# Decode attention on one core: the value loads move from SyncE's queue to GpSimd's

## The chip, the core and the metric

The kernel runs on one core of a Trainium2 chip. The metric is the device time of one execution in microseconds. Three runs of the kernel before gave 1303.39, 1303.53 and 1303.58 us; the median is 1303.53 us. One execution was profiled. The engines are called as the profile calls them: PE (TensorE, matrix products), PEld (its weight loads), DVE (VectorE), ACT (ScalarE), POOL (GpSimd) and SP (SyncE, which here only issues transfers). A "q" behind a name (SPq, ACTq) is that engine's instruction queue, where transfers are issued.

## The reference

One decoding step of grouped-query attention for two tokens, gated by a small MLP; all tensors are 32-bit floats.

```python
xn = layernorm(x)                                   # x: 2 x 1 x 512
q  = (xn @ wq) -> 2 x 32 heads x 128
k, v = caches of 2 x 8 key heads x 32768 x 128, each used by 4 query heads
p  = softmax(q k^T / sqrt(128));  o = p v
s  = o.reshape(2, 4096) @ wo                        # 4096 x 512
g  = silu(relu(xn @ w1 + b1)**2 @ w2 + b2)          # 512 -> 1792 -> 512
out = x + s * g
```

The caches are nearly all of the data: 16 streams (batch x key head) of 16.8 MB of keys and as much of values, 537 MB of the 561 MB that the core reads.

## The kernel before

**Tiling.** A stream s (of 16) has 32768 keys. Its keys K come as two loads of 8.4 MB and its values V as two loads of 8.4 MB, each 128 partitions of 65,536 bytes in one run. Load m of the keys and load j of the values are numbered over all streams, 0 to 31; stream s owns 2s and 2s+1 of both. Every key load is worked through in two quarters q (4 to a stream).

**Buffers.** `kring` has three slots of 32 KB a partition. A key load takes two neighbouring slots: even loads slots 0 and 1, odd loads slots 1 and 2. So the next key load may start when the quarter in the shared slot 1 has been read, which is always the first quarter to be worked on: `load_k(m)` waits for the mark `transposed(2m-2)`. `vbuf` holds a single value load: `load_v(j)` waits until PE has read all of load j-1 (semaphore `pv`, counted by `PV`).

**Work of a quarter.** DVE transposes it from `kring` into `kt` in two instructions (line 309). PE multiplies each half by the masked query `qz` into `ps_s` (line 270). ACT copies the scores out to `sc` (line 333).

**Work of a stream.** After four quarters DVE adds the parts and takes the maximum (line 315), PE spreads it (line 288), DVE makes the bias (line 318), ACT takes the exponential (line 336), PE transposes the probabilities into `pT_ps` (line 299) and ACT copies them to `pTh` (line 343). Then PE multiplies the values by them into `o_ps` (line 280). Values are consumed one stream after their keys.

**Order on each engine.** PE runs a loop over s from 1 to 15: scores of the first two quarters of stream s, values 2s-2, scores of the last two quarters, values 2s-1, then the maximum (288), the transposition of the finished output of stream s-1 (292) and the probabilities (299). It is in order: nothing passes a wait. DVE runs four quarters of transposes, then the maximum, the bias, the sum of the output (485), its reduction (328) and its scaling into `ho` (329), then the sums for the next stream (321, 322). The bias waits for PE, and PE comes to it only after values 2s-1. So the transposes of stream s+1 stand behind values 2s-1.

POOL has two small pieces in a stream: `keep(s-1)`, which copies `ho` into `oT` (line 493) and waits for DVE's line 329, and `set_q(s+1)`, which makes the next masked query (line 246).

**Transfers.** All large loads are issued by SP (line 84, a helper), in program order: weights and the first keys, then in turn a key load and a value load. Each issue stands behind its wait, and the next issue behind it. At the end the last pair of value loads goes to `kring` and to `vbuf`, and the pieces of `wo` to `kring`.

Of the kernel before, what the change touches and what calls it, by code (L numbers as in the profile page):

```python
# [52 lines left out]
def gqa_decode_kernel(nc, x, kc, vc, wq, wo, w1, b1, w2, b2, out):  # L53
# [17 lines left out]
    def sb(name, *shape):  # L71
        return nc.alloc_sbuf_tensor(name, (P,) + shape, F32).ap()

    def bank(name, n=1):
# [3 lines left out]
    SP, ACT, DVE, POOL, TE = (Lane(nc, e, n) for e, n in (  # L78
        (nc.sync, "sp"), (nc.scalar, "act"), (nc.vector, "dve"), (nc.gpsimd, "pool"), (nc.tensor, "pe")))
    tensor, vector, scalar, gpsimd, sync = nc.tensor, nc.vector, nc.scalar, nc.gpsimd, nc.sync  # L80

    def load(lane, dst, src, sem, *marks):
        lane.wait(*marks)
        return sem.after(lane.eng.dma_start(dst, src))  # L84

    def dma(name):
        return Count(nc, name, 16)

    kring = sb("kring", 3 * SLOT, DH)
    vbuf = sb("vbuf", RUN, DH)  # L90
    kt = [sb(f"kt{y}", SLOT, 64) for y in range(2)]

    def rows(cache, s):
        hkv, b = divmod(s, B)
        return cache[b, hkv]
# [5 lines left out]
    def v_rows(j):  # L101
        s, u = divmod(j, 2)
        return rows(vc, s)[u * P * RUN:(u + 1) * P * RUN].rearrange("(p r) d -> p r d", p=P)
# [11 lines left out]
    v_sem = dma("v")  # L115
    KT = [Count(nc, f"kt_{y}") for y in range(2)]
    PA = [Count(nc, f"pa_{y}") for y in range(2)]
    PV = Count(nc, "pv")
# [8 lines left out]
    def load_k(m):  # L127
        a = m % 2
        return load(SP, kring[:, a * SLOT:(a + 2) * SLOT, :], k_rows(m), k_sems[a], transposed(max(2 * m - 2, -1)))
# [114 lines left out]
    def set_q(s):  # L244
        hkv, b = divmod(s, B)
        return POOL(lambda: gpsimd.tensor_tensor(
            qz.rearrange("p e (x h) -> p e x h", h=REP),
            qT[:, b, hkv].rearrange("p h e -> p e h")[:, :, None, :].to_broadcast([P, 4, 8, REP]),
            bm[:, None, :, None].to_broadcast([P, 4, 8, REP]), op=ALU.mult),
            *((have_qT, have_bm) if s == 0 else (PA[1].at(4 * s + 1),)), on=QZ if s else None)  # L250
# [143 lines left out]
    mlp_done = t  # L394

    def load_v(j):
        load(SP, vbuf, v_rows(j), v_sem, PV.at(j) if j else mlp_done)

    load_v(0)
    load_k(3)  # L400
    load_v(1)

    first_keys(3)
    first_scores(3)
# [86 lines left out]
    def keep(s):  # L491
        hkv, b = divmod(s, B)
        return POOL(lambda: gpsimd.tensor_copy(oT[:, b, hkv * REP:(hkv + 1) * REP], ho), (HO.sem, s + 1))  # L493

    for s in range(1, NS):
        for m in (2 * s, 2 * s + 1):
            if m + 2 < NH:
                load_k(m + 2)
                load_v(m)
        kept = keep(s - 1)  # L500
        if s + 1 < NS:
            set_q(s + 1)


    L = NH - 2
# [110 lines left out]
```

## Time and profile before

| | before |
|---|---|
| median of 3 runs | 1303.53 us (1303.39 to 1303.58) |
| span of the profiled execution, first to last instruction | 1302.6 us, 0.93 us under the median |
| busy share of the span: PE, DVE, ACT, POOL | 49%, 48%, 10%, 1% |
| busy share of the 16 DMA engines | 99.6% in SP's queue |
| read from memory | 561.01 MB, 431 GB/s over the span |
| granted clock of PE, mean | 0.785 |

Busy time is the sum of an engine's instructions; issuing and waiting are not counted. The share of a DMA queue is the time that its packets took on 16 DMA engines. A packet here is the run of one partition (65,536 bytes for a key or value load) or a small completion. In a row of the timeline the columns are the start in us, the duration in us, engine, line, operation, what it writes and reads with the tile's size, the count of merged instructions, and in brackets the idle time of the engine ahead of it with what ended it.

### The profile page before, as it was taken

How to read it: one execution, taken by the hardware profiler on the slowest of the kernel's cores; microseconds unless marked ns; L12 is line 12 of the kernel's file. 1: busy time of each engine (PE TensorE's matmuls, PEld its weight loads, DVE VectorE, ACT ScalarE, POOL GpSimd, SP SyncE). 2: the span in 40 equal slices, each digit the busy share in tenths (PEclk: the TensorE clock that was granted, in tenths of full speed). 3: DMA queues.
4: the chain of work that ended last, by engine and by line, in shares of the span. 5: the costliest groups of instructions: out<-in, count | busy, mean ns of one | idle time of the engine just before them, and what ended most of it. 6: DMA issues, size and time to landing. Idle time of an engine off the chain costs nothing.

```text
span 1302.6 us, 10806 instructions
## 1 busy us (share of the span) xinstructions
PE 639.7 (49%) x4710; PEld 175.6 (13%) x4710; DVE 619.0 (48%) x305; ACT 128.6 (10%) x262; POOL 11.9 (1%) x41
## 2 busy tenths in 40 slices
PE   3555444555535455544536543444653444554368
PEld 1111110111101011110101111111110111111014
DVE  2565553436555344655435555343655534455410
ACT  0111011111001011000111101011100101101010
POOL 0000000000000000000000000000000000000000
PEclk9778677878767787777788777678877778877789
DMA  9999999999999999999999999999999999999998
GB/s 419 418 448 423 441 427 435 431 437 433 431 437 427 443 427 441 429 441 427 439 427 437 433 431 437 427 443 427 441 429 441 427 439 427 439 431 429 441 425 356
DMA packets 10703, 561.14 MB, mean 431 GB/s; under 512 B 1199, under 2 KB 1219, under 8 KB 1478
## 3 DMA queue, kind: packets, MB, share of 16 engines
q1 hardware_dynamic: 10656, 560.99, 99.6%
q8 instruction: 6, 0.10, 0.0%
q10 hardware_dynamic: 38, 0.02, 0.0%
q14 instruction: 3, 0.02, 0.0%
HBM read 561.01 MB, written 0.00 MB: 431 GB/s over the span
## 4 chain that ended last, share of the span: by engine, by line
DMA 77%; DVE 12%; issue 10%; PE 1%; SPq 0%; DVEq 0%
DMA kring<-in_A_k_cache 73%; DVE kt L309 12%; DMA kring<-in_A_v_cache 2%; DMA kring<-in_A_wo 2%; PE o_ps L280 1%; PE acc_ps L533 0%; PE pj_ps L540 0%; SPq L84 0%; DVEq L308 0%; PE acc_ps L411 0%
## 5 line engine op out<-in xcount | busy, mean ns | idle before, releaser
L309 DVE STREAM_TRANSPOSE kt<-kring 128x4096 f32<-128x4096 f32 x128 | 557.6, 4414 | 449.4 <-DMA kring<-in_A_k_cache 449.4
L270 PE MATMUL ps_s<-kt,qz 128*32 128x512 f32 x2048 | 333.5, 779 | 603.4 <-DVE kt L309 603.4
L280 PE MATMUL o_ps<-vbuf,pTh 128*16 128x512 f32 x1984 | 227.5, 612 | 1.8 <-DMA vbuf<-in_A_v_cache 1.8
L270 PEld LDWEIGHTS ps_s<-kt,qz 128*32 128x32 f32 x2048 | 67.8, 128 | 845.1 <-issue 669.9
L333 ACT ACTIVATE sc<-ps_s,halves 128x512 f32<-128x512 f32 x64 | 46.6, 729 | 866.5 <-PE ps_s L270 866.5
L280 PEld LDWEIGHTS o_ps<-vbuf,pTh 128*16 128x16 f32 x1984 | 57.8, 101 | 178.0 <-issue 158.6
L343 ACT COPY pTh<-pT_ps 64x256 f32<-64x256 f32 x128 | 46.9, 366 | 39.6 <-PE pT_ps L299 21.6
L315 DVE CUSTOM_DVE_ANT_0 sc<-sc 128x1024 f32<-128x1024 f32 x16 | 19.6, 1225 | 54.9 <-ACT sc L333 54.9
L318 DVE CUSTOM_DVE_ANT_0 junk<-mx_ps,other 128x128 f32<-128x128 f32 x16 | 4.7, 292 | 82.1 <-PE mx_ps L288 82.1
L336 ACT ACTIVATE sc<-sc,nm 128x1024 f32<-128x1024 f32 x16 | 18.4, 1149 | 108.9 <-DVE nm L318 108.9
L328 DVE TENSOR_REDUCE hr<-fin_ps 128x4 f32<-128x64 f32 x16 | 3.6, 225 | 48.5 <-PE fin_ps L292 48.5
L292 PE MATMUL fin_ps<-ident,o_sb 128*128 128x128 f32 x64 | 10.5, 286 | 17.4 <-DVE o_sb L485 17.2
L348 ACT COPY o_sb<-o_ps 128x512 f32<-128x512 f32 x15 | 8.8, 586 | 97.2 <-PE o_ps L280 97.2
L299 PE MATMUL pT_ps<-ident,sc 128*128 128x128 f32 x128 | 17.5, 282 | 0.0
L299 PEld LDWEIGHTS pT_ps<-ident,sc 128*128 128x128 f32 x128 | 15.3, 147 | 0.0
L280 PE MATMUL o_ps<-kring,pTh 128*16 128x512 f32 x64 | 9.3, 749 | 9.0 <-DMA kring<-in_A_v_cache 9.0
L493 POOL COPY oT<-ho 128x4 f32<-128x4 f32 x15 | 2.8, 188 | 1147.2 <-DVE ho L329 1147.2
L210 PE MATMUL pT_ps<-vbuf,xnT 128*32 128x512 f32 x64 | 8.5, 693 | 7.4 <-DMA vbuf<-in_A_wq 7.4
L227 DVE COPY kt<-pT_ps 128x512 f32<-128x512 f32 x8 | 5.0, 683 | 13.2 <-PE pT_ps L210 13.2
L540 PE MATMUL pj_ps<-ident 128*128 128x128 f32 x88 | 10.8, 278 | 0.0
L540 PEld LDWEIGHTS pj_ps<-ident 128*128 128x128 f32 x88 | 10.1, 192 | 1.9 <-issue 1.9
L485 DVE TENSOR_TENSOR o_sb<-o_sb,o_ps 128x512 f32<-128x512 f32 x15 | 10.2, 682 | 0.0
(90 smaller groups left out, 105.5 us busy)
## 6 DMA issues: line engine op xcount, KB each, us to landing
kring<-in_A_k_cache SPq DMA_DIRECT2D x4, 4096.0 KB, 23.8
vbuf<-in_B_w SPq DMA_DIRECT2D x2, 3584.0 KB, 28.5
kring<-in_A_wo SPq DMA_DIRECT2D x1, 4096.0 KB, 41.2
kring<-in_A_wo SPq DMA_DIRECT2D x1, 2304.0 KB, 25.5
kring<-in_A_wo SPq DMA_DIRECT2D x1, 1024.0 KB, 27.6
kring<-in_A_wo SPq DMA_DIRECT2D x1, 512.0 KB, 28.4
vbuf<-in_A_v_cache SPq DMA_DIRECT2D x31, 30.1
kring<-in_A_k_cache SPq DMA_DIRECT2D x30, 29.8
```

The costliest lines, as they stand in the source:

```text
L270: i = tensor.matmul(ps_s[32 * g:32 * g + 32, :], qz[:, 2 * y + e, :], kt[y][:, g * NO:(g + 1) * NO, 32 * e:32 * e + 32], start=(y == 0 and ...
L280: mm_ = tensor.matmul(o_ps[32 * g:32 * g + 16, :], pTh[:, 2 * g + c, 2 * i:2 * i + 2, :, :].rearrange("p o y h -> p (o y h)"), vt[:, lo:lo ...
L292: t = tensor.transpose(fin_ps[:, i * P:(i + 1) * P], o_sb[:, i * DH:(i + 1) * DH], ident)
L299: t = tensor.transpose(pT_ps[:, k // 4, (k % 4) * P:(k % 4 + 1) * P], p[:, k * P:(k + 1) * P], ident)
L309: KT[y].after(vector.transpose(kt[y], k_slot(q)[:, :, 64 * y:64 * y + 64]))
L315: return DVE(lambda: vector.tensor_tensor_reduce(scf[0], scf[0], scf[1], 1.0, -3.4e38, ALU.add, ALU.max, rm), mark, on=on)
L333: ACT(lambda: scalar.mul(sc[c][:, :, :, u], ps_s.rearrange("p (o w) -> p o w", w=32), halves[:, c:c + 1]), *marks, on=EV)
L336: return ACT(lambda: scalar.activation(scf[0], scf[0], AF.Exp, bias=nm, scale=SCALE, accum_out=l), mark, on=on)
L343: i = scalar.copy(pTh[64 * a:64 * a + 64, :, :, y, :], v[64 * y:64 * y + 64, :, :, a0, a, :])
L348: scalar.copy(o_sb, o_ps).then_inc(OE.sem, 32)
L485: DVE(lambda: vector.tensor_add(o_sb, o_sb, o_ps), on=OSR)
L540: tensor.matmul(pj_ps[:, 0:P], ident, ident, start=True, stop=True)
```

## The change

Value loads 0 to 29 are issued from POOL's instruction queue instead of SP's; SP keeps the key loads, the last pair of value loads and the weights. The waits are the same ones: a value load still waits until `vbuf` has been read, a key load until its slots have been read. What is new is that neither queue stands behind the other's waits, and that the value loads stand in POOL's program order, at two places: value load 2s-1 ahead of `keep(s-1)`, and value load 2s behind `keep(s-1)` and `set_q(s+1)`.

```diff
     def load_v(j):
-        load(SP, vbuf, v_rows(j), v_sem, PV.at(j) if j else mlp_done)
+        load(POOL, vbuf, v_rows(j), v_sem, PV.at(j) if j else mlp_done)
 
     load_v(0)
     load_k(3)
-    load_v(1)
...
     for s in range(1, NS):
+        load_v(2 * s - 1)
         for m in (2 * s, 2 * s + 1):
             if m + 2 < NH:
                 load_k(m + 2)
-                load_v(m)
         kept = keep(s - 1)
         if s + 1 < NS:
             set_q(s + 1)
+            load_v(2 * s)
```

SP's order where the steady part begins, before. `kring<-in_A_k_cache` is a key load, `vbuf<-in_A_v_cache` a value load, `vbuf<-in_B_w` a weight of the MLP.

```order
5 L84 DMA vbuf<-in_B_w 128x7168
6 L84 DMA kring<-in_A_k_cache 128x8192 x2
7 L84 DMA vbuf<-in_A_v_cache 128x16384
8 L84 DMA kring<-in_A_k_cache 128x16384
9 L84 DMA vbuf<-in_A_v_cache 128x16384
10 L84 DMA kring<-in_A_k_cache 128x16384
11 L84 DMA vbuf<-in_A_v_cache 128x16384
12 L84 DMA kring<-in_A_k_cache 128x16384
```

And now, up to the end of the streams:

```order
5 L84 DMA vbuf<-in_B_w 128x7168
6 L84 DMA kring<-in_A_k_cache 128x8192 x2
7 L84 DMA kring<-in_A_k_cache 128x16384 x29
8 L84 DMA kring<-in_A_v_cache 128x16384
9 L84 DMA vbuf<-in_A_v_cache 128x16384
10 L84 DMA kring<-in_A_wo 128x8192
```

The strict turn of keys and values is gone from SP: 29 key loads follow one another, each with its own wait.

POOL's order over the first streams, the difference (lines of the kernel after are one less behind the edit). `qz<-qT,bm` is `set_q`, `oT<-ho` is `keep`.

```order
 L246 TENSOR_TENSOR qz<-qT,bm 128x128
-L422 MEMSET oR 128x1024
+L84 DMA vbuf<-in_A_v_cache 128x16384
+L421 MEMSET oR 128x1024
 L246 TENSOR_TENSOR qz<-qT,bm 128x128
-L493 COPY oT<-ho 128x4
+L84 DMA vbuf<-in_A_v_cache 128x16384
+L492 COPY oT<-ho 128x4
 L246 TENSOR_TENSOR qz<-qT,bm 128x128
-L493 COPY oT<-ho 128x4
+L84 DMA vbuf<-in_A_v_cache 128x16384 x2
+L492 COPY oT<-ho 128x4
```

In a steady stream POOL now has `keep`, `set_q`, value load 2s, value load 2s+1, and again `keep`: the even load stands behind two pieces of work, the odd one directly behind the even one.

## The prediction

> **What bounds the kernel now.** First the page: busy shares, the DMA queues, the chain that ended last.
>
> ```profile
> span 1302.6 us, 10806 instructions
> PE 639.7 (49%) x4710; PEld 175.6 (13%) x4710; DVE 619.0 (48%) x305; ACT 128.6 (10%) x262; POOL 11.9 (1%) x41
> ...
> q1 hardware_dynamic: 10656, 560.99, 99.6%
> ...
> DMA 77%; DVE 12%; issue 10%; PE 1%; SPq 0%; DVEq 0%
> ```
>
> No engine is half busy, while the 16 DMA engines work 99.6% of the span in one queue, SP's (q1). The chain runs through key loads and the transposes that free their slots, but that chain is not tight: the bound is the queue. The timeline of one steady stream shows the turn of keys and values:
>
> ```profile
> 408.89 17.43 DVE L309 STREAM_TRANSPOSE kt<-kring 128x4096 f32<-128x4096 f32 x4 [7.82 <-DMA kring<-in_A_k_cache]
> ...
> 417.69 0.33 SPq L84 DMA_DIRECT2D kring<-in_A_k_cache  x1
> ...
> 428.19 7.06 PE L280 MATMUL o_ps<-vbuf,pTh 128*16 128x512 f32 x64
> ...
> 435.31 0.33 SPq L84 DMA_DIRECT2D vbuf<-in_A_v_cache  x1
> ...
> 447.59 17.42 DVE L309 STREAM_TRANSPOSE kt<-kring 128x4096 f32<-128x4096 f32 x4 [21.27 <-DMA kring<-in_A_k_cache]
> ...
> 466.89 0.12 PEld L280 LDWEIGHTS o_ps<-vbuf,pTh 128*16 128x16 f32 x4 [0.81 <-DMA vbuf<-in_A_v_cache]
> ...
> 475.61 0.33 SPq L84 DMA_DIRECT2D vbuf<-in_A_v_cache  x1
> ...
> 486.29 4.45 DVE L309 STREAM_TRANSPOSE kt<-kring 128x4096 f32<-128x4096 f32 x1 [7.79 <-DMA kring<-in_A_k_cache]
> ```
>
> Keys land at 408.89, 447.59 and 486.29, values between them at 428.19 and 466.89. Four loads take 486.29 - 408.89 = 77.4 us, so one takes **T = 19.35 us**, and nothing lies between them. A key load is issued at 417.69 and its bytes can start only at 428.19, when the values have landed: 10.5 us early. A value load is issued at 435.31 and starts at 447.59: 12.3 us early. So "as soon as its own buffer is free" removes no idle DMA time: what stands behind a wait on SP is a transfer that could not have run.
>
> **What the change removes.** Thirty issues of 0.33 us on SP, none on a path, and the strict turn of the two kinds. In one queue a load that comes late costs nothing as long as the other one, at full rate, lasts T. That cover is what the change gives up. With two queues the engines share, and whichever load ends first leaves of the other less than T.
>
> **How the engines share** is the first thing that no steady part of this trace shows. The start shows a little of it: ACT issues the small load of x while SP's first load streams.
>
> ```profile
> 0.74 0.38 SPq L84 DMA_DIRECT2D vbuf<-in_A_wq  x1
> ...
> 1.43 1.22 ACTq L84 DMA_DIRECT2D kt<-in_A_x  x1
> ...
> 10.34 0.69 DVE L188 TENSOR_REDUCE st<-kt 128x1 f32<-128x512 f32 x1 [7.33 <-DMA kt<-in_A_x]
> ...
> 22.90 8.52 PE L210 MATMUL pT_ps<-vbuf,xnT 128*32 128x512 f32 x64 [7.38 <-DMA vbuf<-in_A_wq]
> ```
>
> SP's load is seen at 22.90, that is 22.16 after its issue; less T this leaves **2.8 us** for start and receipt of a load. Alone, x would have been there at 1.43 + (1.22 - 0.38) + 2.8 = 5.1. It came at 10.34: 5.3 us late, but 12.6 us before the load ahead of it. So the engines change queues inside a load. A load has 128 runs, 8 to each engine, so a packet is T/8 = **2.4 us**, and 5.3 us are about two packets: one ahead of the data, one ahead of the completion behind it. I take turns of one packet each.
>
> [...]
>
> **The gaps.** Call a gap the time in which a kind of load moves no bytes: from its last byte to the first of its next one. What sets them in the second half of a stream:
>
> ```profile
> 467.41 8.14 PE L280 MATMUL o_ps<-vbuf,pTh 128*16 128x512 f32 x64
> ...
> 478.14 0.19 POOL L493 COPY oT<-ho 128x4 f32<-128x4 f32 x1 [76.81 <-DVE ho L329]
> 478.28 0.47 POOL L246 TENSOR_TENSOR qz<-qT,bm 128x128 f32<-128x128 f32 x1
> 478.32 0.18 DVE L322 RECIPROCAL rl<-lh 128x4 f32<-128x4 f32 x1
> ```
>
> - Keys: two transposes, 417.69 - 408.89 = 8.8, and 2.8: 11.6 us.
> - Values 2s-1, the odd ones, behind values 2s-2: 435.31 - 428.19 = 7.1, and 2.8: 9.9 us, and e for POOL's way of issuing.
> - Values 2s, the even ones: before, they were issued at 475.61. Now they stand behind `keep` and `set_q`, which ends at 478.75. From landing (466.89) this is 11.9, and 2.8: 14.7 us, and e. The 3.1 us that the order on POOL adds were covered by the 12.3 us of lead.
> - DVE comes to the next stream's transposes at 478.50, 11.6 us after values 2s-1 have landed, however early the keys are there.
>
> **e**, what a transfer issued from POOL takes longer than one from SP, is the second unknown: POOL issues none before. From below: it cannot win more than SP's own issue row, -0.33. From above: as much again as all of a load's start and receipt, 2.8. I take 0.5, by the nearest row, a POOL instruction (0.47). [...]
>
> **One stream, step by step.** Values 2s-1 land at time L. Values 2s are issued at L + 11.9 and the next keys at L + 11.6 + 8.8 = L + 20.4. So the values run alone for 8.5 - e, and half a packet more until the keys get their first turn, 1.2: together 9.7 - e. From there both run at half rate, and when the values end the keys have as much left as the values had ahead: 9.7 - e. The completion of the values stands behind one packet of the keys, 2.4. The gap of the odd values is then 9.9 + e + 2.4 = 12.3 + e, and the keys cover 9.7 - e of it: **idle 2.6 + 2e**. Now the odd values run alone; keys come back 11.6 + 1.2 after they ended, so the values are ahead by 12.8 - 2.6 - 2e = 10.2 - 2e. That is again what the keys have left when the values end, against a gap of 14.7 + e + 2.4: **idle 6.9 + 3e**. By then DVE is behind values 2s+1 again, and the next stream starts in the same position: the loss doesn't grow, and it doesn't heal.
>
> Sum: 9.5 + 5e in a stream, 12.0 us with e = 0.5. Value loads 2 to 29 are 14 such streams: 168 us. The span becomes 1302.6 + 168 = 1470.6, and with the 0.9 us by which the median lies above the profiled span, **1471 us**.
>
> The ends: with no wait for the completion (turns far shorter than a packet would leave neither that nor the half packets) the sum is 5.9 + 5e, at e = 0 83 us: 1386. With the half packets but no wait for the completion and e = 0 the idle times are 0.2 and 2.1, 32 us: 1336; at e = -0.33, 0.6 us in a stream, 1312. At e = 2 it is 19.5 a stream, 273 us: 1577. At e = 2.8 it meets the cap that the lockstep below gives. The forecast's own range is 1315 to 1577.
>
> Small things go to nothing. `keep` and `set_q` stand behind the odd value load's wait, which PE lets go before DVE makes `ho`. The tail (last values, `wo`) has its waits unchanged and the transfers in the same order.
>
> **Rivals.**
>
> *Whole loads in turn, not slower (0.17).* If an engine drains what it has begun, the two queues act as one: a gap of at most 14.7 + e lies under a transfer of 19.35. The place is the even value load, whose 3.1 + e us of delay come out of 12.3 us of lead; it decides as long as what the keys have left exceeds the gap. The time is that of before, 1303.5, perhaps 1 to 4 us more from the start. For it: the covers are long, and the packets of POOL's queue may be framed otherwise. Against it: x came 12.6 us before the load ahead of it.
>
> *Lockstep (0.14).* If keys get more than half of the turns, or POOL is held up, both kinds of load end together and both gaps lie open: 11.6 us for each pair, 29 pairs, 336 us: 1640. For it: values 2s are issued at L + 11.9, just as DVE begins transposes at L + 11.6; were POOL held for the first of them (4.4 us), the even gap alone would take idle to about 20 us in a stream, 1580. [...] Against it: no row of POOL shows such a hold, though none runs beside a transpose either.
>
> *Faster (0.04).* Engines with two queues could pass from packet to packet without the 0.4% that they now don't work: 5 us, 1298. Against it: that 0.4% is mostly start and end, where both kernels wait alike.
>
> **How the numbers follow.** The forecast holds 0.65 and gives 1471. The range runs from 1303, so that the whole-load case is in it, to 1580; left out are most of the lockstep, half of what the forecast has at its upper end, and the faster case: some 0.18. This kernel's runs lie within 0.02%, but about 0.2% is what a measurement can tell from no change, 2.6 us. Faster by more: 0.04. The same: 0.13 of the whole-load case. Slower: the rest, 0.83.
>
> **What would show it.** Right: the busy share of DMA falls to about 0.89, PE, DVE and ACT have the same busy times as before, keys are issued 8.8 us after their first transpose starts and odd values 7.1 to 8.7 us after. Landing times of keys and values, now 19.35 us apart, come close, with holes in the DMA's slices just before a value load starts; a stream takes 89.4 us for 77.4. The even value load is issued about 12 us after its forerunner landed, and loads take about 29 us from the first byte to the last, as they share. Wrong: value loads that land in about 22 us with the key loads' bytes standing still meanwhile (whole loads in turn); a value load that makes no way while keys move (lockstep); POOL's issue long after its wait was met (e too small); or a DMA share of 99% at a longer time, which would be a lower rate of two mixed streams and not idle time, a cost for which I count nothing.

## The result, and the profile after

The kernel with the change takes 1429.45 us (median of 4 runs, 1427.44 to 1432.39) beside 1303.49 us for the kernel before on the same chip. The ratio is 1.0967, interval 1.0954 to 1.0980: slower by 126.0 us, where 167.5 us were forecast (range 1303 to 1580). Some runs of the experiments below fell into a slower state of the chip; the ratios leave these out, the medians and ranges hold them.

The page of the kernel after:

```profile
span 1428.3 us, 10806 instructions
PE 680.6 (48%) x4710; PEld 176.2 (12%) x4710; DVE 619.0 (43%) x305; ACT 127.8 (9%) x262; POOL 28.3 (2%) x71
...
q1 hardware_dynamic: 6336, 309.33, 50.2%
q0 software_dynamic: 4320, 251.66, 42.0%
...
DMA 73%; PE 21%; DVE 3%; issue 1%; POOL 1%; ACT 0%; DVEq 0%; SPq 0%
...
L280 PE MATMUL o_ps<-vbuf,pTh 128*16 128x512 f32 x1984 | 276.7, 720 | 342.7 <-DMA vbuf<-in_A_v_cache 342.7
```

The queues together are busy 92.2% of 1428.3 us, that is 1317 us; before it was 99.6% of 1302.6, that is 1297. So about 106 us of the 126 are idle time of the DMA engines, and about 20 us are packets recorded as longer. In the chain of waits PE now has 21% (1% before). Its products with the values (line 280) wait for values for 342.7 us in all and take 276.7 us: each value load waits for products, and they for the load.

One steady stream of the kernel after, in its timeline, from one even value load to the next:

```profile
702.40 0.60 POOL L84 DMA_DIRECT2D vbuf<-in_A_v_cache  x1
702.47 17.42 DVE L309 STREAM_TRANSPOSE kt<-kring 128x4096 f32<-128x4096 f32 x4 [0.28 <-issue]
...
711.27 0.33 SPq L84 DMA_DIRECT2D kring<-in_A_k_cache  x1
...
734.32 9.12 PE L280 MATMUL o_ps<-vbuf,pTh 128*16 128x512 f32 x64 [12.44 <-DMA vbuf<-in_A_v_cache]
...
743.81 0.53 POOL L84 DMA_DIRECT2D vbuf<-in_A_v_cache  x1 [40.81 <-PE o_ps L280]
744.03 17.42 DVE L309 STREAM_TRANSPOSE kt<-kring 128x4096 f32<-128x4096 f32 x4 [24.14 <-DMA kring<-in_A_k_cache]
...
752.83 0.33 SPq L84 DMA_DIRECT2D kring<-in_A_k_cache  x1
...
775.53 9.00 PE L280 MATMUL o_ps<-vbuf,pTh 128*16 128x512 f32 x64 [11.21 <-DMA vbuf<-in_A_v_cache]
...
787.68 0.59 POOL L84 DMA_DIRECT2D vbuf<-in_A_v_cache  x1
```

The period is 787.68 - 702.40 = 85.28 us for 77.40 before: 7.9 us more. The two holes of the prediction are there. When the odd value load is issued at 743.81, the keys have just landed (744.03), and nothing moves until that load's bytes start. With the 2.8 us of start and receipt: 743.81 + 2.8 - 744.03 = **2.6 us**. The other 7.9 - 2.6 = **5.3 us** lie before the even load that is issued at 787.68.

The same in the stretches of the trace. The columns are the window, its length, busy time of PE, PEld, DVE, ACT and POOL with counts, PE's granted clock, DMA share and GB/s. Short windows of DMA swing with the long packets, and a single zero also stands in other places; what counts is a zero just ahead of a load's first packets. First the kernel after:

```profile
702.40:787.68 85.28, 39.85 (x272) 9.43 (x270) 37.76 (x17) 7.51 (x15) 1.69 (x5) 0.76 0.92 393
...
742.00:744.00 2.00, 1.44 (x16) 0.20 (x8) 0.00 (x0) 0.43 (x1) 0.19 (x1) 1.00 0.00 0
...
774.00:776.00 2.00, 0.47 (x4) 0.15 (x8) 0.00 (x0) 0.00 (x0) 0.00 (x0) 0.50 1.21 524
...
778.00:780.00 2.00, 2.00 (x16) 0.45 (x12) 0.00 (x0) 0.00 (x0) 0.00 (x0) 0.63 1.21 524
780.00:782.00 2.00, 2.00 (x24) 0.54 (x20) 0.00 (x0) 0.00 (x0) 0.00 (x0) 1.00 0.30 131
...
784.00:786.00 2.00, 0.85 (x10) 0.20 (x3) 0.90 (x3) 0.69 (x1) 0.00 (x0) 1.00 0.00 0
786.00:788.00 2.00, 1.79 (x13) 1.31 (x13) 1.02 (x5) 0.71 (x3) 0.89 (x3) 1.00 0.00 0
788.00:790.00 2.00, 0.00 (x0) 0.00 (x0) 2.00 (x1) 1.31 (x4) 0.27 (x1) 0.93 1.53 524
```

And a stream of the kernel before:

```profile
408.89:486.29 77.40, 36.75 (x270) 9.42 (x270) 37.76 (x17) 7.56 (x15) 0.62 (x2) 0.79 1.00 434
```

The DMA share of a stream falls from 1.00 to 0.92. From 742 to 744, ahead of the odd value load, nothing moves, and from 784 to 788, ahead of the even one, nothing again: the keys have landed and wait to be transposed, the values have been used up, and POOL is busy with its two small pieces. The first packets behind that hole are recorded longer for the same bytes (1.53 where a full stretch has 1.21, both at 524 GB/s), and there I put the 20 us above, which no run tested. The rows also show what the prediction left out: PE is idle ahead of the products, its clock stands at 0.50 when they begin, and comes back to 1.00 only some 4 us later (0.63 in the mean of 778 to 780).

**Where the 126 us lie.** From the issue of value load 2 to that of load 28, 13 streams, it was 1172.27 - 166.04 = 1006.23 us before and is 1299.76 - 190.81 = 1108.95 us now: 102.7 us more, 7.9 in each stream. Ahead of load 2 it is 190.81 - 166.04 = 24.8 us more, and behind load 28 it is 1.8 us less. Sum: 125.7. The first and the last of these issues, after:

```profile
190.81 0.59 POOL L84 DMA_DIRECT2D vbuf<-in_A_v_cache  x1
...
1299.76 0.60 POOL L84 DMA_DIRECT2D vbuf<-in_A_v_cache  x1
```

And before:

```profile
166.04 0.33 SPq L84 DMA_DIRECT2D vbuf<-in_A_v_cache  x1
...
1172.27 0.33 SPq L84 DMA_DIRECT2D vbuf<-in_A_v_cache  x1
```

### The profile page after: what moved, and what is told of

Same layout as the page of the kernel before. It is cut to its first block, busy times and chain, and to the rows that moved or that the text cites. A ratio compares the mean times of both kernels' runs of the same rounds, so it can differ in the third digit from the quotient of the medians.

```text
span 1428.3 us, 10806 instructions
## 1 busy us (share of the span) xinstructions
PE 680.6 (48%) x4710; PEld 176.2 (12%) x4710; DVE 619.0 (43%) x305; ACT 127.8 (9%) x262; POOL 28.3 (2%) x71
## 3 DMA queue, kind: packets, MB, share of 16 engines
q0 software_dynamic: 4320, 251.66, 42.0%
## 4 chain that ended last, share of the span: by engine, by line
DMA 73%; PE 21%; DVE 3%; issue 1%; POOL 1%; ACT 0%; DVEq 0%; SPq 0%
DMA vbuf<-in_A_v_cache 66%; PE o_ps L280 19%; DMA kring<-in_A_k_cache 7%; DVE kt L309 2%; PE fin_ps L292 1%; DVE o_sb L484 1%; PE pj_ps L525 0%; POOL qz L246 0%; DVE junk L318 0%; PE mx_ps L288 0%; DVE hr L328 0%; POOL oT L492 0%; DVE ho L329 0%; PE ps_s L270 0%; PE acc_ps L533 0%
## 5 line engine op out<-in xcount | busy, mean ns | idle before, releaser
L270 PE MATMUL ps_s<-kt,qz 128*32 128x512 f32 x2048 | 321.9, 755 | 356.4 <-DVE kt L309 354.6
L280 PE MATMUL o_ps<-vbuf,pTh 128*16 128x512 f32 x1984 | 276.7, 720 | 342.7 <-DMA vbuf<-in_A_v_cache 342.7
L280 PEld LDWEIGHTS o_ps<-vbuf,pTh 128*16 128x16 f32 x1984 | 58.8, 111 | 572.4 <-DMA vbuf<-in_A_v_cache 382.4
L84 POOL DMA_DIRECT2D vbuf<-in_A_v_cache x30 | 17.0, 568 | 670.4 <-PE o_ps L280 621.8
L292 PE MATMUL fin_ps<-ident,o_sb 128*128 128x128 f32 x64 | 10.5, 286 | 17.4 <-DVE o_sb L484 17.2
## 6 DMA issues: line engine op xcount, KB each, us to landing
kring<-in_A_k_cache SPq DMA_DIRECT2D x4, 4096.0 KB, 34.2
kring<-in_A_wo SPq DMA_DIRECT2D x1, 512.0 KB, 29.3
vbuf<-in_A_v_cache POOLq DMA_DIRECT2D x30, 31.9
```

The source lines that it names most:

```text
L270: i = tensor.matmul(ps_s[32 * g:32 * g + 32, :], qz[:, 2 * y + e, :], kt[y][:, g * NO:(g + 1) * NO, 32 * e:32 * e + 32], start=(y == 0 and ...
L280: mm_ = tensor.matmul(o_ps[32 * g:32 * g + 16, :], pTh[:, 2 * g + c, 2 * i:2 * i + 2, :, :].rearrange("p o y h -> p (o y h)"), vt[:, lo:lo ...
L292: t = tensor.transpose(fin_ps[:, i * P:(i + 1) * P], o_sb[:, i * DH:(i + 1) * DH], ident)
```

## The experiments

The theory: two queues cost what the gaps leave uncovered. While one kind of load waits for its buffer, only the other one can move bytes, and of that one less is left than a whole load. The rivals for the size are that POOL's way of issuing is slow, that two queues mixed run at a lower rate, and that the start is a loss of its own.

### Is it GpSimd's way of issuing, or two queues as such?

**All loads through POOL, in one queue.** The key loads from 2 on and value loads 0 to 29 are issued by POOL in strict turn; `keep` and `set_q` stand between them (diff against the kernel before, shortened).

```diff
-        return load(SP, kring[:, a * SLOT:(a + 2) * SLOT, :], k_rows(m), k_sems[a], transposed(max(2 * m - 2, -1)))
+        return load(POOL if m > 1 else SP, kring[:, a * SLOT:(a + 2) * SLOT, :], k_rows(m), (p_sems if m > 1 else k_sems)[a], transposed(max(2 * m - 2, -1)))
...
-        load(SP, vbuf, v_rows(j), v_sem, PV.at(j) if j else mlp_done)
+        load(POOL, vbuf, v_rows(j), v_sem, PV.at(j) if j else mlp_done)
...
     for s in range(1, NS):
-        for m in (2 * s, 2 * s + 1):
-            if m + 2 < NH:
-                load_k(m + 2)
-                load_v(m)
+        if s + 1 < NS:
+            load_k(2 * s + 2)
+            load_v(2 * s)
         kept = keep(s - 1)
         if s + 1 < NS:
             set_q(s + 1)
+            load_k(2 * s + 3)
+            load_v(2 * s + 1)
```

> Key loads 2 to 31 and value loads 0 to 29 all go through POOL's one queue, in the strict turn of the kernel before; keep and set_q stand between them. So everything passes by POOL's way of issuing, and nothing shares. Gap theory: each gap lies under a whole load of the other kind, 1303 to 1308 us. Path theory (POOL's transfers cost more or run slower): 64 loads at 0.5 us or more each, 1335 us or above.

Measured: 1306.56 us (1304.9 to 1307.5), ratio 1.0024 (1.0013 to 1.0034). Its page:

```profile
q0 software_dynamic: 8928, 503.32, 89.3%
q1 hardware_dynamic: 1872, 57.67, 10.3%
```

90% of the bytes go through POOL's queue and together with SP's queue the engines are busy 99.6% of the span. The forecast of the gaps was 1303 to 1308 us, that of a slow path 1335 or more. POOL's path and its program order together cost 3.0 us (1.7 to 4.4 by the interval). The path is not what the change pays for.

**The values on ACT's queue instead, with the even load as late as in the change.** In ACT's order it stands behind the copies of the probabilities.

```diff
-        load(POOL, vbuf, v_rows(j), v_sem, PV.at(j) if j else mlp_done)
+        load(ACT, vbuf, v_rows(j), v_sem, PV.at(j) if j else mlp_done)
...
             if u == 0:
+                load_v(2 * s - 1)
                 act_o((PV.sem, 2 * s - 1))
                 act_probs(1)
         act_exp((NM.sem, s), EXP)
         act_probs(0, (PPR.sem, s))
+        if s + 1 < NS:
+            load_v(2 * s)
```

> Value loads on ACT's queue again, with value load 2s behind the copies of the probabilities (line 343), whose wait is over some 12 us after values 2s-1 landed when their products take 9 us, as late as the load on POOL in the change. In the run before on ACT the load went out at the start of the exponential, 7.85 us after landing. Gap theory: the lateness makes the loss, whoever issues: 1390 to 1435 us, DMA share 0.92 to 0.95. Path theory: as on ACT before, 1314 to 1339 us.

Measured: 1428.63 us (1427.8 to 1432.2), ratio 1.0969 (1.0950 to 1.0987), the time of the change. Its timeline:

```profile
701.49 0.34 ACTq L84 DMA_DIRECT2D vbuf<-in_A_v_cache  x1
...
732.89 9.47 PE L280 MATMUL o_ps<-vbuf,pTh 128*16 128x512 f32 x64 [12.10 <-DMA vbuf<-in_A_v_cache]
...
742.43 0.33 ACTq L84 DMA_DIRECT2D vbuf<-in_A_v_cache  x1
...
774.16 9.31 PE L280 MATMUL o_ps<-vbuf,pTh 128*16 128x512 f32 x64 [12.15 <-DMA vbuf<-in_A_v_cache]
...
786.80 0.33 ACTq L84 DMA_DIRECT2D vbuf<-in_A_v_cache  x1
```

It is the change's stream again (85.3 us) without POOL in it. From issue to landing the even load takes 31.4 us here and 31.9 in the change, the odd one 31.7 in both. So e, the extra of POOL's path, lies between 0 and 0.5 us by these two loads.

**The values on ACT's queue, with the even load ahead of those copies**, behind the exponential in the program.

```diff
         act_exp((NM.sem, s), EXP)
+        if s + 1 < NS:
+            load_v(2 * s)
         act_probs(0, (PPR.sem, s))
```

> Value loads 0 to 29 go through ACT's queue instead of POOL's (ACT's loop is written out). The even load stands behind the exponential (line 336), so that it comes about 12 us after its forerunner landed, as on POOL; the odd one directly behind its wait. Gap theory: the second queue is what counts and not whose it is: 1420 to 1440 us, DMA share 0.92. Path theory: with transfers that are issued like SP's the loss goes away: 1304 to 1330 us.

Measured: median 1326.73 us of runs of 1313.9, 1316.4, 1337.1 and 1339.0, for which there is no interval. The profile is of the first. The edit did not do what it was meant to; its timeline:

```profile
713.41 7.06 PE L280 MATMUL o_ps<-vbuf,pTh 128*16 128x512 f32 x64 [0.59 <-DMA vbuf<-in_A_v_cache]
...
721.26 1.15 ACT L336 ACTIVATE sc<-sc,nm 128x1024 f32<-128x1024 f32 x1 [7.65 <-DVE nm L318]
721.26 0.33 ACTq L84 DMA_DIRECT2D vbuf<-in_A_v_cache  x1
```

The transfer is issued just as the exponential ahead of it begins, 7.9 us after the products began, where it was meant to come as late as in the change. So it became a test of two queues without lateness. From value load 2 on:

```profile
179.35:1188.09 1008.74, 504.79 (x3510) 124.02 (x3510) 490.83 (x222) 97.98 (x196) 7.99 (x26) 0.75 1.00 433
```

Those 13 streams take 77.6 us each, at a DMA share of 1.00 and 433 GB/s (434 in the kernel before). Two mixed queues are as fast as one. The run before this one differs in the place of the even load alone: there it is issued 786.80 - 774.16 = 12.6 us after the products begin, 4.8 us later than here. Of these, 2.3 are the products themselves, which take 9.3 us there and 7.06 here. The medians lie 102 us apart, the single runs 89 to 118.

### Are the gaps the price?

**The even value load ahead of POOL's two pieces.** One change of order on POOL.

```diff
+        if s + 1 < NS:
+            load_v(2 * s)
         kept = keep(s - 1)
         if s + 1 < NS:
             set_q(s + 1)
-            load_v(2 * s)
```

> Only POOL's program order is changed: value load 2s stands ahead of keep(s-1) and set_q(s+1). Gap theory (the loss is idle DMA time where the gap of the values is longer than what the keys have left): with the numbers of the changed kernel's trace the even gap falls from 12.15 + 2.8 to about 9.5 + 2.8 us, the values of stream s start 2.7 us earlier against the keys, and both idle times of a stream go to about 0 (from 2.65 and 5.25). What is left is the start, about 23 us: 1326 us, DMA share 0.98 or more. Path theory (transfers from POOL, or two mixed queues, are slower in themselves): the 2.7 us are won at most once in a stream, 14 x 2.7 = 38 us: 1391 us.

Measured: 1341.30 us (1333.4 to 1351.3), ratio 1.0303 (1.0241 to 1.0365). Moving two POOL instructions, of 0.65 us together, from ahead of one load to behind it is worth 88 us of the 126, for the load had waited 3.1 us with them for DVE. Timeline and window:

```profile
767.41 8.75 PE L280 MATMUL o_ps<-vbuf,pTh 128*16 128x512 f32 x64 [7.10 <-DMA vbuf<-in_A_v_cache]
...
776.50 0.59 POOL L84 DMA_DIRECT2D vbuf<-in_A_v_cache  x1 [35.61 <-PE o_ps L280]
```

```profile
182.82:1212.68 1029.86, 523.09 (x3510) 122.87 (x3510) 491.00 (x222) 97.64 (x195) 22.66 (x52) 0.78 0.99 424
```

A stream takes 1029.86 / 13 = 79.2 us, 1.8 more than before the change. The even gap is now 776.50 - 767.41 = 9.1 us and the start, for the 9.5 of the expectation. Both holes were to go to about nothing and the time to 1326 us; that it stayed 15 us above is a miss. PE still waits 7.1 us ahead of the products and takes 8.75 us for them.

**Both value loads later.** POOL writes a spare tile four times ahead of each value load from 1 on, once the buffer is free.

```diff
+        t = ()
+        if j:
+            POOL.wait(PV.at(j))
+            for _ in range(4):
+                t = (POOL(lambda: gpsimd.memset(pad, 0.0), *t),)
-        load(POOL, vbuf, v_rows(j), v_sem, PV.at(j) if j else mlp_done)
+        load(POOL, vbuf, v_rows(j), v_sem, *t, PV.at(j) if j else mlp_done)
```

> Ahead of each value load from 1 on, behind its wait, POOL writes a small spare tile four times, about 1 us. Gap theory: each microsecond by which both value loads come later costs 5 us in a stream (1 + 1 directly, and 3 more because the keys come nearer to the values and cover less of the next gap): 14 x 5 = 70 us, 1500 us. Path theory: each load comes 1 us later and no more, 28 x 1 = 28 us: 1457 us.

Measured: 1572.13 us (1570.1 to 1573.4), ratio 1.2058 (1.2038 to 1.2079). Timeline:

```profile
712.49 0.98 POOL L403 MEMSET pad<- 128x128 f32 x4 [43.09 <-PE o_ps L280]
713.78 0.53 POOL L84 DMA_DIRECT2D vbuf<-in_A_v_cache  x1 [0.30 <-POOL pad L403]
...
750.51 9.44 PE L280 MATMUL o_ps<-vbuf,pTh 128*16 128x512 f32 x64 [18.93 <-DMA vbuf<-in_A_v_cache]
...
763.11 0.98 POOL L403 MEMSET pad<- 128x128 f32 x4
764.67 0.60 POOL L84 DMA_DIRECT2D vbuf<-in_A_v_cache  x1 [0.58 <-POOL pad L403]
```

The loads are 1.3 and 1.6 us later. The period from value load 2 to 28 is (1433.62 - 190.67) / 13 = 95.6 us, 10.3 more than in the change. Five times the mean delay, as the sum has it, is 7.1. So lateness is multiplied as forecast, and by more than forecast: 1572 us for 1500. Some 2 of the other 3 us are in the landings. The odd load lands 750.51 - 713.78 = 36.7 us after its issue, 5.0 later than in the change, and the even one after 34.2, 2.3 later, while their lead over the keys shrank by 3.5 and 1.6 us. Landings move in steps of about 2.4 us, as shown below.

**The keys later.** They wait for one more transpose, 4.4 us, which a theory of lateness alone would call a loss.

```diff
-        return load(SP, kring[:, a * SLOT:(a + 2) * SLOT, :], k_rows(m), k_sems[a], transposed(max(2 * m - 2, -1)))
+        return load(SP, kring[:, a * SLOT:(a + 2) * SLOT, :], k_rows(m), k_sems[a], KT[0].at(2 * m) if m > 2 else transposed(max(2 * m - 2, -1)))
```

> Only one wait is changed: key loads from 3 on wait for one transpose more (the first of the next quarter), so each is issued 4.4 us later. Gap theory: what covers the gap of the values is the lead with which they started before the keys; each microsecond by which the keys come later adds to that lead and takes 3 us from the idle time of a stream (1 from the first hole, 2 from the second), so 4.4 us are more than enough for 7.9: no steady loss, 1305 to 1325 us, DMA share 0.98 or more. Any theory in which the loads are slow in themselves, or the keys' chain sets the time: no gain, 1429 us or more, up to 29 x 4.4 = 128 us more.

Measured: 1358.49 us (1354.6 to 1362.7), ratio 1.0413 (1.0382 to 1.0444): 71 us of the 126 come back by making a load wait longer. A value load that is alone for 4.4 us more ends earlier against the keys (27.9 us from issue to landing in the median, 31.9 in the change), and more of the keys is left to cover the values' gap. A stream takes (1234.17 - 189.31) / 13 = 80.4 us between the issues of value loads 2 and 28. It was to come to 1305 to 1325 us and did not. Timeline and a window:

```profile
722.97 17.42 DVE L309 STREAM_TRANSPOSE kt<-kring 128x4096 f32<-128x4096 f32 x4 [26.26 <-DMA kring<-in_A_k_cache]
...
736.10 37.77 SPq L84 DMA_DIRECT2D kring<-in_A_k_cache  x2
...
742.19 7.05 PE L280 MATMUL o_ps<-vbuf,pTh 128*16 128x512 f32 x64
```

```profile
735.00:737.00 2.00, 0.78 (x8) 0.34 (x12) 2.00 (x2) 0.07 (x1) 0.00 (x0) 1.00 0.00 0
```

The products begin without a wait and at full clock (7.05 us); over the whole run they wait 23.7 us for values, for 342.7 in the change. So the values' holes are nearly closed. What remains, and what the expectation had left out, is a hole on the other side: the values have landed, nothing moves from 735 to 737, and the keys are issued at 736.10, 13.1 us after the first transpose.

**Both of these edits**, the keys later and the even value load earlier.

> The later keys and POOL's order with value load 2s ahead of keep and set_q, together. Gap theory: nothing is left that either could cover, so within a few us of the later keys alone, 1304 to 1320 us. If each took its own part of the loss: clearly faster than either.

Measured: 1339.27 us (1336.8 to 1377.0), ratio 1.0256 (1.0235 to 1.0276) from the three shorter runs. It is 19 us faster than the later keys alone, not within a few us as expected, and no faster than the order alone beyond the scatter. So with the order changed, the later keys fill nothing more: the two edits fill the same holes, and the order does it without the hole on the keys' side.

**The same edit of the keys in the kernel before.**

> The kernel before, with one queue, and the same edit of the keys' wait: each key load from 3 on is issued 4.4 us later. Gap theory: in one queue a key load is issued 10.5 us before its bytes can start, so 4.4 us come out of a lead and cost nothing: 1303.4 to 1304.0 us. If the issue times of the keys set the time, as the chain of waits of the kernel before reads (DMA into kring and the transposes follow one another in it): up to 29 x 4.4 = 128 us more.

Measured: 1303.59 us (1303.3 to 1304.0), ratio 1.0000 (0.9991 to 1.0010). In one queue 4.4 us come out of a lead of 10.5 and cost nothing. This is the cover that the prediction named, tested by itself.

### PE's slower products

**Spare products ahead of the values.** PE multiplies a constant tile by itself 36 times into a tile that nobody reads, before each wait for values, to keep its clock up.

```diff
+            with nc.Fori(0, 9, 1, engines=[PE]):
+                for _ in range(4):
+                    tensor.matmul(pj_ps[:, 0:P], ident, ident, start=True, stop=True)
             for c in (v_sem, PTH, OE):
```

> PE runs 36 spare products (results unused) while it waits for each value load, so that it stays busy; nothing on the queues is touched. In the changed kernel the products with values take 9.1 us behind 12 us of idle PE, before the change 7.06. Gap theory: both gaps fall by about 2 us; idle times 0.65 and 1.2 instead of 2.65 and 5.25, 1.85 us in a stream: 1430 - 14 x 6 = 1345 us. Path theory: 2 us a load at most, 28 x 2 = 56 us: 1373 us. If the slower products are not a matter of idle PE: no change, 1430 us.

Measured: 1448.60 us (1433.0 to 1451.8), ratio 1.1072 (1.1011 to 1.1134). No gain, but 19 us lost on the change, and the timeline says why nothing was won:

```profile
704.40 9.58 PE L280 MATMUL o_ps<-vbuf,pTh 128*16 128x512 f32 x64 [7.12 <-DMA vbuf<-in_A_v_cache]
```

Here the spare products end 7.1 us before the values land. By then the clock is back at 0.50, as the last window ahead of the landing shows, and the products take 9.6 us:

```profile
702.00:704.00 2.00, 0.00 (x0) 0.00 (x0) 0.00 (x0) 0.00 (x0) 0.00 (x0) 0.50 1.21 524
```

**More of them**: 11 rounds for 9, 44 products.

> The changed kernel with 44 spare products on PE ahead of each wait for values, not 36: with 36 PE still sat idle for 2.5 to 7 us before the values and its granted clock was 0.50 when they began, and they took 9.3 to 9.6 us. With 44 the clock should be at 0.8 or above when they begin. If the slow start of the values is the clock's: products of 7.1 to 8 us, gaps 1.5 us shorter, some 4.5 us in a stream: 1367 us. If not: 9 us and 1430 to 1450 us.

Measured: 1415.38 us (1412.4 to 1416.1), ratio 1.0851 (1.0833 to 1.0869). Timeline and group:

```profile
738.90 8.76 PE L280 MATMUL o_ps<-vbuf,pTh 128*16 128x512 f32 x64 [2.42 <-DMA vbuf<-in_A_v_cache]
...
779.68 7.06 PE L280 MATMUL o_ps<-vbuf,pTh 128*16 128x512 f32 x64 [1.65 <-DMA vbuf<-in_A_v_cache]
```

```profile
L280 PE MATMUL o_ps<-vbuf,pTh 128*16 128x512 f32 x1984 | 232.8, 624 | 58.8 <-DMA vbuf<-in_A_v_cache 58.6
```

With 58.8 us of waiting in all, 1.9 us for each group of 64, the products take 232.8 us for 276.7. A stream takes (1286.48 - 204.87) / 13 = 83.2 us between the issues of value loads 2 and 28, so 2.1 of the 7.9 us went away with the clock. That is about half of the 4.5 that I had expected, and the start of the kernel, 14 us longer up to value load 2, took half of it back: 1415 us, where 1367 were expected. In places the spare work itself may hold the values up. The sign is shown; the full 4.3 us a stream that I put down to the slower products (below) is not.

### The start

**Value load 0 waits for key load 2**, so that the two don't share the engines at the start.

```diff
-        load(POOL, vbuf, v_rows(j), v_sem, PV.at(j) if j else mlp_done)
+        load(POOL, vbuf, v_rows(j), v_sem, *((PV.at(j),) if j else (mlp_done, k_sems[0].at(3))))
```

> Value load 0 on POOL waits, beside its own wait, until key load 2 has landed, as it does in one queue; all else as in the change. Gap theory: in the changed kernel key load 2 and value load 0 land together and key load 3 can only be issued 8.8 us later, which with what follows puts value load 2 24.8 us later than before; with this wait some 5 us of the start are left: 1410 us. If the start were only the first of the steady losses: no more than 8 us won, 1421 us or above.

Measured: 1431.18 us (1428.3 to 1435.1), ratio 1.0977 (1.0952 to 1.1003): the time of the change. Timeline:

```profile
99.54 0.72 POOL L84 DMA_DIRECT2D vbuf<-in_A_v_cache  x1 [63.75 <-DMA kring<-in_A_k_cache]
...
133.92 9.14 PE L280 MATMUL o_ps<-vbuf,pTh 128*16 128x512 f32 x64 [14.89 <-DMA vbuf<-in_A_v_cache]
```

Value load 0 now shares with key load 3 instead of key load 2 and lands 34 us after its issue. Value load 2 is issued at 190.47, for 190.81 in the change. The sharing only moved, and my idea of the start, which gave 1410 us, fell.

**This edit and the order on POOL together.**

> Both edits: value load 2s ahead of keep and set_q, and value load 0 behind the landing of key load 2. Gap theory: the run with the order alone left 38 us, of which 16.8 lie ahead of value load 2; some 12 of these go: 1329 us. If the two losses are one: no better than 1341 us.

Measured: 1357.69 us (1341.0 to 1367.7), ratio 1.0321 (1.0282 to 1.0361) from the two shorter runs, 1341.0 and 1349.9 us, no better than the order alone. It says the same.

No run with values in a queue of their own is as fast as the kernel before. The fastest of those with an interval is 2.6% slower; the fastest single run, 1313.9 us, 0.8%.

## Why the prediction was right, and where its sum was not

**Right: what bounds, and what is given up.** The DMA engines are the bound (99.6% busy in SP's queue before the change), SP's waits hid nothing that could have run, and one queue covers a late load by a whole load of the other kind. In one queue 4.4 us of lateness of the keys cost nothing; with two, 3.1 us of lateness of the even value load cost 88 us.

**Right: the holes and their places.** Two in each stream, each just ahead of a value load. The keys were issued 8.8 us after the first transpose, as forecast, and the even load 787.68 - 775.53 = 12.15 us after its forerunner landed (11.9). POOL's issues of 0.53 to 0.60 us stand right beside DVE's transposes (702.40 and 702.47), so nothing held POOL up and the lockstep fell. The busy times of DVE and ACT are those of before; PE's are not.

**Wrong: the wait of the completion behind one packet of the other queue, 2.4 us.** It was to count three times in a stream, 7.2 of the 12.0 us. With it, the forecast's terms make the even load land 2.8 + 0.5 + 38.7 - (8.37 + 1.2) + 2.4 = 34.8 us after its issue (38.7 is 2T, and 8.37 the 8.87 us to the keys' issue less e); it lands after 31.9. Let w be the head start that the turns give the load that began first, and p the wait of the completion. Then 2.8 + e + 38.7 - (8.87 - e + w) + p = 31.9, so w - p = 0.7 + 2e. With the 1.2 that I had for w, p is at most 0.5. The row of the load of x, from which I took "one packet ahead of the data, one ahead of the completion", bears that its data came late, not how the delay is split.

Nor is w - p a constant. Among the value loads that were issued less than 1 us ahead of the keys' landing, or behind it, the time from issue to landing goes in steps. It is 36.6 to 36.8 us where the next keys are issued 4.8 to 5.6 us behind (the run with both value loads later). It is 34.1 to 34.6 us with 7.3 to 8.7 us, and once with 8.8 (that run, and five loads of the runs with 36 spare products and with the later start). It is 31.4 to 32.2 us with 8.7 to 9.4 us (the change and most runs). Each step is about 2.4 us, one packet. The change lies just above an edge: in the run with the later start one load took 34.5 us with the keys 8.66 us behind, another 31.8 with 8.70. So the landings fit turns by whole packets, as forecast, while half a packet for w and a whole one for p made a smooth sum of a stair; below that edge its 34.8 us would have been near.

**Missing: the odd gap grows.** I took 7.1 us from the old trace, in which PE hardly waited for values. Now it waits 11 to 12 us, begins at a clock of 0.50 and takes 9.1 us for the same 64 products, so the odd load is issued 743.81 - 734.32 = 9.5 us after the landing, above the 8.7 that the prediction allowed. With the measured terms and 0.7 for w - p, hole one is (9.5 + 2.8) - 8.9 - 0.7 = 2.7 us. The odd load's lead over the next keys is 752.83 + 2.8 - 746.6 = 9.0, and hole two is (12.15 + 2.8) - 9.0 - 0.7 = 5.2 us. That their sum is the 7.9 us of the period is bookkeeping, since these issues and landings are its parts. What tests the terms are two times from which none was taken: the odd load should land 2.8 + 38.7 - 9.0 - 0.7 = 31.8 us after its issue and lands after 31.7, and the keys should land at 702.40 + 2.8 + 38.7 = 743.9 and do so at 744.03. The first hole came out near its forecast (2.6 for 3.6) only because 2.4 us too little and some 3.4 too much met in it.

So the sum was 4.1 us a stream too high. With w - p = 0.7 + 2e the forecast's 5.9 + 3p - 3w + 5e is 3.8 - e: some 8.4 us less. The slower products count in both holes, since a first hole that is longer shortens the lead on which the second rests; 2 x 2.4 and small differences of the other gaps bring 4.3 back. That share is argued from the rows; of the two runs with spare products one bears out its sign and about half of its size. That the total came as near as it did is in part luck: 13 streams cost 102.7 us where 14 were to cost 168, and the start, counted as nothing, put 24.8 back.

**At the upper end: e, 0.5.** Beside ACT's queue it lies between 0 and 0.5. From issue to landing the even load takes 31.9 us for 31.4 there, the odd one 31.7 in both, and the 0.5 is the upper of the two.

**Counted as nothing: the start.** It holds 24.8 us of the 126. The first loads share the engines too: key load 2, issued at 80.27 with value load 0 behind it at 85.99, lands only at 118.74, 38.5 us later, where 19.35 + 2.8 = 22.2 would be a load alone. The stretch up to the issue of value load 2 in the kernel after:

```profile
0.00:190.81 190.81, 81.03 (x586) 25.07 (x586) 88.33 (x61) 18.77 (x42) 4.95 (x17) 0.79 0.91 391
```

And the kernel before, up to the same issue:

```profile
0.00:166.04 166.04, 80.03 (x573) 23.57 (x573) 86.66 (x54) 17.59 (x40) 3.07 (x12) 0.80 1.00 429
```

A share of 0.91 leaves some 17 us of DMA idle, where before there was none. The other 7.8 us are no loss. Up to that issue the kernel after has moved 391 GB/s x 190.81 us = 74.6 MB and the kernel before 71.2 MB, and the 3.4 MB between them take 7.8 us at 434 GB/s. So 17.0 us are lost at the start, and behind load 28, where less is left to move, it is 6.0 us lost and not 1.8 won. Which waits set these stays open, since moving value load 0 changed nothing.

**The rivals.** Whole loads in turn fell with the time and with the landings: the even value load takes 31.9 us and not 22. Nor do whole loads in turn fit landings that move in steps of 2.4 us, an eighth of a load. The profile's 4320 packets for POOL's 30 loads are 144 a load, 128 runs and 16 completions. "Faster" was wrong in sign, and its premise, that two queues would win the last 0.4%, was not borne out: two queues moved 433 GB/s in the run where nothing stood idle, one moved 434.

## What to carry to other kernels

When the transfers are the bound and each load waits for its own buffer, a strict turn in one queue is no restraint: it gives every load the whole transfer ahead of it as cover, here 19.35 us against gaps of 10 to 15. Before splitting such loads over two queues, add up each kind's gap (its last byte to its next first byte) and compare it with what the other kind has left at that moment, not with a whole transfer. Ask then which engine will newly be idle ahead of its work, and time its work as it runs from a standstill, here 9.1 us for 7.06.

## What the runs showed that I had not expected

- **The clock fell in PE's waits and lengthened a buffer's hold.** In the change's stream above PE has no work from 721.9 us, where its scores end, to 734.3; its clock is 1.00 in the mean of 722 to 724, 0.72 of 724 to 726 and 0.50 of 726 to 728. In the rows above 64 products take 8.8 to 9.6 us after 2.4 to 14.9 us without work, and 7.06 after 0.59 and 1.65 us. Behind the 2.42 us the clock stood at 1.00 as the products began and was at 0.54 from 740 to 742. The wait alone doesn't set it: the kernel before has 8.14 us behind one of 0.81. In the trace of the change it is 0.50 at the products' start and 1.00 some 4 us into them. So a hole makes the next one larger: the odd load is issued 9.5 us after the landing, for 7.1 before the change.
- **A later load can make a faster kernel.** 4.4 us more of waiting for the keys brought 71 us.
- **Near balance the runs scatter.** With both kinds of load on queues of their own and small holes, runs of one kernel lie 1% apart (1333 to 1351 us with the order changed), while kernels with one queue for both agree within 0.2%. A landing that slips is one candidate: in the profiled run with the order changed a single load took 34.2 us from issue to landing, where the others in the steady streams took 29.3 to 30.2. What tips them was not tried.
